# A new instruction order for a fused attention and gated-MLP block: logit sums in pairs, output projection last in three blocks

## The chip, the cores and the metric

The kernel runs on one core of one Trainium2 chip. The metric is the device time of one execution in microseconds (us). Three runs of the kernel before took 180.56, 180.65 and 180.72 us; the median is 180.65 us. The profiled execution is a run of its own and took 180.63 us, of which 179.4 us lie between its first and its last instruction (the span).

## The reference

The input x has 2048 positions of 512 features in bf16. Two branches read the same layer norm and are added to x:

```python
x = A_x
xn = _layernorm(x, axis=-1)
return x + _A_ref(xn, A_wqkv, A_wo) + _B_ref(xn, B_w_gate, B_w_up, B_w_down)
```

Branch A is attention with 32 heads of 16 features in which each position looks at itself and at seven positions behind it, two apart (`off = jnp.arange(8) * 2`); positions before the start are masked. After the softmax over the eight places and the weighted sum of v comes the projection with `wo` (512 x 512). Branch B is a gated MLP, `gelu(xn @ w_gate) * (xn @ w_up) @ w_down`, with 1376 hidden features.

## The kernel before

The 2048 positions are cut into four blocks (0 to 3) of 512 positions and sixteen tiles of 128. For each block the same tasks exist, and a task's name carries the block number:

- **Layer norm.** Blocks 0 and 1 mostly on VectorE (DVE), blocks 2 and 3 on ScalarE (ACT). The result xnT is transposed to [feature, position].
- **q, k, v** (`mm1_0_3_0` is block 1, q, group 3): four matmuls of 512 columns each on TensorE (PE) into one bank of PSUM; ACT copies the bank to SBUF (`evq`, `evk`, `evv`, L1029).
- **Attention logits.** DVE multiplies q with the eight shifted copies of k (`pr`, L1049, two instructions of 8192 elements per partition) and adds them up part of the way (`pa`, `pb`). The rest of the sum over features is done by PE with a 0/1 matrix: the task `er` (L1097), the *logit sums*. It works on 32 columns of the array at a time and also makes the last small part of the up projection (L1085), whose two results ACT copies out as `uev_10b` and `uev_10c` (L1292).
- **Softmax.** ACT copies the logits to SBUF (`lc`, L1120); DVE takes the maximum and subtracts it (`d1a` to `d1c`, `d2`); ACT takes the exponential (`exp`, L1143); DVE sums (`d4a` to `d4c`, L1151); ACT takes the logarithm (`ln`, L1161) and the exponential of its negative (`d5`, L1165), which is the reciprocal; DVE multiplies (`d6`, L1169). Four DMAs store the weights to a scratch tensor in HBM (`ss`) and four load them back spread over the heads (`sl`).
- **Weighted sum of v** on DVE (`pv`, L1199, `pw`, `pz`): `pz` writes the attention output OT of the block.
- **Gate and up projections** (`fg`, `fu`, ten pieces each and a rest): four matmuls of 512 columns into a bank; ACT reads the gate through gelu (`gelu`, L1247) and copies the up part (`uev`, L1254); DVE multiplies both (`h`, L1261) into HT.
- **Output** of each tile: one bank collects four matmuls OT x Wo and eleven HT x Wd (L1329). The parts are named `acca`, `accb`, `accd` (the Wd ones) and `accw` (the four Wo ones by themselves). With `WO_LAST` holding a block, the Wo matmuls of that block come at the end of the sum, as a task of their own; else they come at its start and the whole sum waits for `pz`. ACT copies the bank to the buffer OB (`fe`, L1362), DVE adds x (`fin`), a DMA stores (`sto`). In the last two tiles DVE reads the bank itself.

The order of the tasks on each engine is not found at run time: the table `ORDER` lists them by name, and the function `schedule` only deals out buffer slots in that order and the semaphore waits follow from the data. Each engine runs its list strictly in order. So do the DMAs, which all stand in the list of one queue, SP's. PSUM has eight banks in one pool; a matmul task waits until the bank that it is given has been read out.

ACT holds one set of function tables at a time. The line `e.preload_act_table_set("natural_log_exp_and_others")` (L1142) stands ahead of each `exp` and puts an instruction ACT_TABLE_LOAD there in every case; that set has the exponential and the logarithm. All other loads are put in when the program is built, where a function follows that is not in the set loaded last: for gelu, for `ln` and for `d5`. Plain copies (Identity) need none. In `schedule`, a switch is charged where the `table` of a task (`"gelu"`, `"exp"`) differs from the one before:

```python
G.task("act", "ln%d" % b, 0.21, mk_ln(), rd=[(it_ms, 0)], wr=[(it_ms, 0)], prio=base + 34, table="exp")
```

Of the kernel before, what the change touches and what calls it, by code (L numbers as in the profile page):

```python
# [96 lines left out]
class Graph:  # L97
# [251 lines left out]
    def report(self):  # L349
# [14 lines left out]
ORDER = {  # L364
# [14 lines left out]
    "act":  # L379
# [17 lines left out]
    "dve":  # L397
# [9 lines left out]
    "pool":  # L407
        "c_ones c_onef c_id c_vnpad c_idb c_eps c_mhalf c_e8a c_e8b c_e8c c_e8d c_ktpad c_mask0 c_mask1 c_utz sq8 "
# [9 lines left out]
}  # L418


# [16 lines left out]
def bass_parallel_sum__sliding_local_dilated__glu_gated_geglu__prompt_kernel(nc, A_x, A_wqkv, A_wo, B_x, B_w_gate, B_w_up, B_w_down, out, dbg=None, cfg=None):  # L437
    cfg = dict(cfg or {})
# [6 lines left out]
    JT = cfg.get("JT", 4.5)  # L445
    JLATE = cfg.get("JLATE", [8, 9])
    NMS = cfg.get("NMS", 1)
    NPB = cfg.get("NPB", 1)
    NPT = cfg.get("NPT", 4)
    NVN = cfg.get("NVN", 2)  # L450
    NOT = cfg.get("NOT", 2)
# [1 line left out]
    NHT = cfg.get("NHT", 2)  # L453
    NXR = cfg.get("NXR", 2)
    XRB = cfg.get("XRB", 2)
    NOB = cfg.get("NOB", 4)
    NDMASEM = cfg.get("NDMASEM", 24)
    QUOTAS = cfg.get("QUOTAS", dict(tp=2, qkv=2, lg=2, o=4, ffn=3,
                                    acc=2, acl=4))
# [7 lines left out]
    PPOW = cfg.get("PPOW", 4)  # L467
    FIN2 = cfg.get("FIN2", tuple(range(14)))
    PR_ADD3 = cfg.get("PR_ADD3", (0, 1, 2, 3))
    WO_LAST = cfg.get("WO_LAST", (3,))  # L470
    CHAIN_SHIFT = cfg.get("CHAIN_SHIFT", [0, 300, 600, 900])
    FFN_BASE = cfg.get("FFN_BASE", 500)
    FFN_STEP = cfg.get("FFN_STEP", 1000)
# [2 lines left out]
    NB, NP, NT = 4, 8, 16  # L476
    NJ = 11
    x2 = A_x[0]
    out2 = out[0]

    with contextlib.ExitStack() as es:
        def sb(name, shape, dt):
# [43 lines left out]
        GG = sb("GG", [128, NGG, 2, 512], BF)  # L526
# [3 lines left out]
        OB = sb("OB", [128, NOB, 512], BF)  # L530
        PS = es.enter_context(nc.psum_tensor("PS", [128, 4096], F32))
# [23 lines left out]
        P_gg = Pool("gg", NGG)  # L555
# [3 lines left out]
        P_ob = Pool("ob", NOB)  # L559
# [34 lines left out]
            out=cf[:, :], in_=cf[:, :], pattern=[[-1, 128]], compare_op=ALU.is_equal, fill=0.0, base=0,  # L594
# [7 lines left out]
            out=E8f[:, :], in_=E8f[:, :], pattern=[[-4, 32]], compare_op=ALU.is_ge, fill=0.0, base=0,  # L602
            channel_multiplier=1), rd=[I_E8f], wr=[I_E8f], prio=PC2)
        G.task("pool", "c_e8c", 0.25, lambda e: e.affine_select(
            out=E8f[:, :], in_=E8f[:, :], pattern=[[4, 32]], compare_op=ALU.is_ge, fill=0.0, base=3,
# [77 lines left out]
        for p in range(NP):  # L683
# [24 lines left out]
            for t2 in range(2):  # L708
                t = 2 * p + t2
# [209 lines left out]
        for b in range(NB):  # L919
# [383 lines left out]
            for ti in range(4):  # L1303
# [15 lines left out]
                for ci, (c0, c1) in enumerate(cparts):  # L1319
                    CW = c1 - c0  # L1320
                    sfx = "%d" % t if len(cparts) == 1 else "%d_%d" % (t, ci)
                    it_acc = Item("acc" + sfx, P_ps, "acl" if b in WO_LAST else "acc")
                    it_ob = Item("ob" + sfx, P_ob, "ob")

                    def mk_acc(ops, start, stop, ti=ti, it=it_acc, ith=it_ht, ito=it_ot, c0=c0, c1=c1, CW=CW):
                        def f(e):
# [33 lines left out]
                    if t in FIN2:  # L1360
# [5 lines left out]
                        def mk_fin(xr_of=xr_of, ito=it_ob):  # L1366
                            return lambda e: e.tensor_tensor(out=OB[:, ito.slot, :], in0=OB[:, ito.slot, :],
                                                             in1=xr_of(0, 512), op=ALU.add)
                        G.task("dve", "fin" + sfx, d_dve(CW, 0.52), mk_fin(), rd=[xrp], wr=[it_ob],
                               prio=base + 61)  # L1370
                    else:
                        def mk_fin(it=it_acc, xr_of=xr_of, ito=it_ob, c0=c0, c1=c1, CW=CW):
                            return lambda e: e.tensor_tensor(
                                out=OB[:, ito.slot, 0:CW], in0=PS[:, 512 * it.slot:512 * it.slot + CW],
                                in1=xr_of(c0, c1), op=ALU.add)
                        G.task("dve", "fin" + sfx, d_dve(CW), mk_fin(), rd=[it_acc, xrp], wr=[it_ob],
                               prio=base + 61)

                    def mk_so(t=t, it=it_ob, c0=c0, c1=c1, CW=CW):
                        return lambda e: e.dma_start(out2[128 * t:128 * t + 128, c0:c1], OB[:, it.slot, 0:CW])  # L1380
                    G.task("sp", "sto" + sfx, 0, mk_so(), rd=[it_ob], wr=[(I_out, (t, ci))], prio=base + 62,
                           nbytes=64 * CW)

# [43 lines left out]
```

## Time and profile before

| | before |
|---|---|
| median of three runs | 180.65 us |
| profiled execution | 180.63 us |
| its span | 179.4 us |
| TensorE (PE) busy | 174.6 us, 97% |
| VectorE (DVE) busy | 169.5 us, 94% |
| ScalarE (ACT) busy | 131.8 us, 73% |
| GpSimd (POOL) busy | 22.6 us, 13% |
| DMA engines, mean share | 37.5% on the one queue of the program |
| granted TensorE clock | 1.00 over the whole span |

Busy shares are means over the whole span. A line of the timeline gives the start and length of a stretch, the engine, the source line, the operation, the tiles (written <- read), the shape and the count; in brackets stands how long the engine was idle before it and what ended that. Consecutive instructions of DVE and ACT overlap in the records by about 0.1 us, so the step from one start to the next is what an instruction costs in a packed row.

### The profile page before, as it was taken

To read this page: it belongs to the slowest core of one execution; us is meant where nothing else is said; L and a number is where in the kernel's file an instruction comes from. 1 tells how busy PE (TensorE), PEld (TensorE's weight loads), DVE (VectorE), ACT (ScalarE), POOL (GpSimd) and SP (SyncE) were. 2 spreads that over 40 slices of the span, in tenths; PEclk is the share of its full clock that TensorE was granted. 3 is DMA by queue.
4 is the path that set the end of the run, shared out by engine and by line. 5 is a ranking of instruction groups with operands and counts; after the bars stand their busy time and mean duration, and the time that the engine had idled before them with its cause. 6 is when DMAs were issued, how large, how long until landed. Compare 5 with 4: busy or idle time off the path is not lost.

```text
span 179.4 us, 2670 instructions
## 1 busy us (share of the span) xinstructions
PE 174.6 (97%) x1007; PEld 88.4 (49%) x1024; DVE 169.5 (94%) x155; ACT 131.8 (73%) x262; POOL 22.6 (13%) x23
## 2 busy tenths in 40 slices
PE   7899999999999999999999999999999999999995
PEld 2797555444454455444444544444444444444453
DVE  3899999999999999999999999999899999999954
ACT  5689999999999999999766888734829796411031
POOL 6000350045000039117000000000000000000000
DMA  4995594640368110003660010053703067400123
GB/s 115 375 384 125 120 329 127 203 169 0 60 180 231 36 23 4 0 11 76 187 140 0 0 58 0 4 151 89 255 3 117 4 116 250 132 0 29 62 88 117
DMA packets 26988, 19.60 MB, mean 109 GB/s; under 512 B 13696, under 2 KB 24800, under 8 KB 26976
## 3 DMA queue, kind: packets, MB, share of 16 engines
q1 hardware_dynamic: 26976, 19.44, 37.5%
q8 instruction: 8, 0.13, 0.3%
q14 instruction: 4, 0.03, 0.1%
HBM read 14.71 MB, written 3.15 MB: 100 GB/s over the span
## 4 chain that ended last, share of the span: by engine, by line
PE 67%; ACT 16%; DVE 11%; DMA 2%; issue 1%; SPq 0%; DVEq 0%
PE PS L1329 25%; PE PS L1237 23%; PE PS L1018 10%; DVE UNI L1199 4%; ACT UU L1254 3%; PE PS L935 3%; ACT GG L1247 3%; DVE UNI L1208 2%; DMA Wqkv<-in_A_wqkv_dram 2%; ACT XS L774 2%; PE PS L993 1%; ACT L1247 1%; PE PS L1276 1%; DVE UNI L1214 1%; PE PS L949 1%
## 5 line engine op out<-in xcount | busy, mean ns | idle before, releaser
L1329 PE MATMUL PS<-Wd,HT 128*128 128x512 bf16 (+2 forms) x185 | 40.2, 366 | 0.1
L1237 PE MATMUL PS<-xnT,Wg 128*128 128x512 bf16 x156 | 38.9, 379 | 0.2
L1237 PE MATMUL PS<-xnT,Wu 128*128 128x512 bf16 x156 | 38.6, 379 | 0.2
L1199 DVE TENSOR_TENSOR UNI<-VN,PT 128x8192 f16<-128x8192 bf16 x8 | 35.4, 4420 | 0.9 <-DMA PT<-pt_scratch 0.9
L1049 DVE TENSOR_TENSOR UNI<-QT,KT 128x8192 f16<-128x8192 bf16 x8 | 35.3, 4418 | 0.0
L1018 PE MATMUL PS<-xnT,Wqkv 128*128 128x512 bf16 x141 | 32.7, 379 | 0.3 <-issue 0.2
L1329 PEld LDWEIGHTS PS<-Wd,HT 128*128 128x128 bf16 x187 | 17.9, 98 | 20.3
L1247 ACT ACTIVATE GG<-PS 128x512 bf16<-128x512 f32 x40 | 23.4, 612 | 5.8 <-DVE HT L1261 3.3
L781 POOL TENSOR_TENSOR sq<-vb,mhalf 128x2 bf16<-128x2 bf16 x4 | 19.7, 4925 | 60.4 <-ACT vb L778 60.4
L1254 ACT ACTIVATE UU<-PS 128x512 bf16<-128x512 f32 x40 | 23.4, 609 | 3.4 <-PE PS L1237 2.1
L1237 PEld LDWEIGHTS PS<-xnT,Wu 128*128 128x128 bf16 x160 | 15.6, 98 | 18.7 <-ACT GG L1247 0.3
L1237 PEld LDWEIGHTS PS<-xnT,Wg 128*128 128x128 bf16 x160 | 15.6, 98 | 18.6 <-ACT XIN L802 0.4
L1362 ACT ACTIVATE OB<-PS 128x512 bf16<-128x512 f32 x14 | 8.1, 593 | 22.4 <-PE PS L1329 20.6
L1018 PEld LDWEIGHTS PS<-xnT,Wqkv 128*128 128x128 bf16 x144 | 16.2, 114 | 15.1 <-ACT QT L1029 0.3
L1061 DVE TENSOR_TENSOR UNI<-UNI 128x8192 f16<-128x8192 f16 x4 | 17.7, 4420 | 0.0
L1208 DVE TENSOR_TENSOR UNI<-UNI 128x8192 f16<-128x8192 f16 x4 | 17.7, 4418 | 0.0
L1329 PE MATMUL PS<-Wo,OT 128*128 128x512 bf16 (+2 forms) x65 | 16.0, 366 | 0.2
L1261 DVE TENSOR_TENSOR HT<-GG,UU 128x1024 bf16<-128x1024 bf16 x20 | 13.4, 684 | 0.0
L1329 PEld LDWEIGHTS PS<-Wo,OT 128*128 128x128 bf16 x68 | 6.4, 98 | 7.6 <-issue 0.4
L1214 DVE TENSOR_TENSOR UNI<-UNI 128x4096 f16<-128x4096 f16 x4 | 9.1, 2286 | 0.0
L1068 DVE TENSOR_TENSOR UNI<-UNI 128x4096 f16<-128x4096 f16 x4 | 9.1, 2282 | 0.0
L1029 ACT ACTIVATE QT<-PS 128x512 bf16<-128x512 f32 x12 | 7.0, 610 | 1.2 <-PE PS L1018 1.2
(97 smaller groups left out, 176.3 us busy)
## 6 DMA issues: line engine op xcount, KB each, us to landing
PT<-pt_scratch SPq DMA_DIRECT2D x16, 256.0 KB, 4.3
out_dram<-OB SPq DMA_DIRECT2D x15, 128.0 KB, 1.7
XIN<-in_A_x_dram SPq DMA_DIRECT2D x12, 128.0 KB, 2.4
Wqkv<-in_A_wqkv_dram SPq DMA_DIRECT2D x3, 512.0 KB, 5.0
XIN<-in_A_x_dram SPq DMA_DIRECT2D x6, 256.0 KB, 5.0
Wg<-in_B_w_gate_dram SPq DMA_DIRECT2D x2, 640.0 KB, 5.9
Wu<-in_B_w_up_dram SPq DMA_DIRECT2D x2, 640.0 KB, 6.6
Wd<-in_B_w_down_dram SPq DMA_DIRECT2D x1, 1280.0 KB, 6.4
```

What stands on the lines that cost most here:

```text
L781: "pool", "sq%d" % t, 6.0, lambda e, t=t, n=n: e.tensor_tensor(out=sq[:, t:t + n], in0=vb[:, t:t + n], in1=mhalf[:, 0:n], op=ALU.pow),
L1018: ins = e.matmul(PS[:, 512 * it.slot:512 * it.slot + 512], lhsT=wcols(which, kt, g), rhs=xnT[:, itx.slot, kt, :], start=(kt == 0), stop=(k ...
L1049: return lambda e: e.tensor_tensor(out=UNI[:, it.slot:it.slot + 2, :, :], in0=bass.AP(QT, (itq.slot * 4 + 2 * h) * 512, [[NQT * 4 * 512, 1 ...
L1061: return lambda e: e.tensor_tensor(out=UNI[:, i0.slot:i0.slot + 2, :, :], in0=UNI[:, i0.slot:i0.slot + 2, :, :], in1=UNI[:, i1.slot:i1.slo ...
L1199: return lambda e: e.tensor_tensor(out=bass.AP(UNI, ito.slot * 4096, [[NUNI * 4096, 128], [2048, 4], [512, 4], [1, 512]]), in0=bass.AP(VN, ...
L1208: return lambda e: e.tensor_tensor(out=UNI[:, i0.slot:i0.slot + 2, :, :], in0=UNI[:, i0.slot:i0.slot + 2, :, :], in1=UNI[:, i1.slot:i1.slo ...
L1214: return lambda e: e.tensor_tensor(out=UNI[:, i0.slot, :, :], in0=UNI[:, i0.slot, :, :], in1=UNI[:, i0.slot + 1, :, :], op=ALU.add)
L1237: ins = e.matmul(PS[0:M, 512 * it.slot:512 * it.slot + 512], lhsT=Wx[:, kt, j * 128:j * 128 + M], rhs=xnT[:, itx.slot, kt, :], start=(kt = ...
L1247: return lambda e: e.activation(out=GG[:, ito.slot, q, :], in_=PS[:, 512 * it.slot:512 * it.slot + 512], func=ACTF.Gelu_apprx_tanh)
L1254: return lambda e: e.activation(out=UU[:, ito.slot, q, :], in_=PS[:, 512 * it.slot:512 * it.slot + 512], func=ACTF.Identity)
L1261: return lambda e: e.tensor_tensor(out=HT[:, ito.slot, j - 1:j + 1, :], in0=GG[:, ig.slot, :, :], in1=UU[:, iu.slot, :, :], op=ALU.mult)
L1329: ins = e.matmul(PS[:, 512 * it.slot:512 * it.slot + CW], lhsT=(OT[:, ito.slot, q, ti * 128:(ti + 1) * 128] if kind == "o" else HT[:, ith. ...
```

## The change

The table `ORDER` is replaced as a whole: the same tasks in another order on PE, ACT, DVE and SP (POOL is unchanged), with eight new tasks `accw0` to `accw7` that come from `WO_LAST`. `NPB` gives the softmax weights PB a second buffer, `NOB` takes one of four output buffers OB away, and the last two tiles write their output into a buffer of the gelu results (GG) in place of OB. No matmul, activation or vector operation is added or left out, apart from table loads.

```diff
-        "evq2_0_0 evq2_1_0 exp1 evq2_3_0 evk2_2_0 evk2_0_0 bnst14 ln1 halv2 bnst15 evk2_3_0 d5_1 uev1_7 sub12 "
+        "uev1_10c va14 uev1_2 exp1 uev1_5 gelu1_2 gelu1_4 gelu1_3 gelu1_5 sub14 norm12 sub15 evv1_2_0 norm13 "
...
-    NPB = cfg.get("NPB", 1)
+    NPB = cfg.get("NPB", 2)
...
-    NOB = cfg.get("NOB", 4)
+    NOB = cfg.get("NOB", 3)
...
-    WO_LAST = cfg.get("WO_LAST", (3,))
+    WO_LAST = cfg.get("WO_LAST", (0, 1, 3))
...
-                    it_ob = Item("ob" + sfx, P_ob, "ob")
+                    it_ob = Item("ob" + sfx, P_gg if t >= NT - 2 else P_ob, "ob")
+                    ob_of = ((lambda c0, c1, it=it_ob: GG[:, it.slot, 0, c0:c1]) if t >= NT - 2 else
+                             (lambda c0, c1, it=it_ob: OB[:, it.slot, c0:c1]))
...
-                                out=OB[:, ito.slot, 0:CW], in0=PS[:, 512 * it.slot:512 * it.slot + CW],
+                                out=ob_of(0, CW), in0=PS[:, 512 * it.slot:512 * it.slot + CW],
...
-                        return lambda e: e.dma_start(out2[128 * t:128 * t + 128, c0:c1], OB[:, it.slot, 0:CW])
+                        return lambda e: e.dma_start(out2[128 * t:128 * t + 128, c0:c1], ob_of(0, CW))
```

The lines of the changed kernel are one to three higher than those of the kernel before (L1143 for L1142, L1255 for L1254, L1332 for L1329).

**PE, the logit sums of blocks 0 and 1.** Before, the sums of block 1 (L1085 and L1097, 32 columns) stand alone among matmuls of 128 columns, as do those of block 0:

```order
L1237 MATMUL PS<-xnT,Wg 128x512 x4
L1085 MATMUL PS<-xnT,Wt 32x256 x16
L1097 MATMUL PS<-UNI,E 32x512 x8
L1237 MATMUL PS<-xnT,Wg 128x512 x4
L1018 MATMUL PS<-xnT,Wqkv 128x512 x8
```

Now those of block 0 (with the mask) are followed at once by those of block 1:

```order
L1019 MATMUL PS<-xnT,Wqkv 128x512 x20
L1086 MATMUL PS<-xnT,Wt 32x256 x16
L1093 MATMUL PS<-mask,const-bfloat16-1.0 32x4x16
L1098 MATMUL PS<-UNI,E 32x512 x4
L1093 MATMUL PS<-mask,const-bfloat16-1.0 32x4x16
L1098 MATMUL PS<-UNI,E 32x512 x4
L1086 MATMUL PS<-xnT,Wt 32x256 x16
L1098 MATMUL PS<-UNI,E 32x512 x8
L1019 MATMUL PS<-xnT,Wqkv 128x512 x4
```

Two entries into the 32-column form and two returns from it became one of each; the same holds for blocks 2 and 3.

**ACT, the exponential of block 1 (`exp1`).** Before, it stands among copies; the logarithm (L1161) and the second exponential (L1165) of the block follow with no gelu and no load between:

```order
L1142 ACT_TABLE_LOAD
L1143 ACTIVATE EX<-PB 128x1024
L1029 ACTIVATE QT<-PS 128x512
L1029 ACTIVATE KT<-PS 128x512 x2
L731 ACTIVATE XS,s<-XIN 128x512
L1161 ACTIVATE ms<-ms 128x128
L1037 ACTIVATE VN<-VN 128x4x16
L731 ACTIVATE XS,s<-XIN 128x512
L1029 ACTIVATE KT<-PS 128x512
L1165 ACTIVATE rc<-ms 128x128
```

Now it stands fifteen ACTIVATEs behind the exponential of block 0, with only copies, layer-norm work, `ln0` and `d5_0` between, and the gelus of block 1 follow:

```order
L1255 ACTIVATE UU<-PS 128x512
L1293 ACTIVATE UT<-PS 32x512
L775 ACTIVATE XS,s<-XIN,nmean 128x512
L796 ACTIVATE XIN<-XIN,nmean 128x512
L1293 ACTIVATE UT<-PS 64x256
L779 ACTIVATE vb<-s,eps 128x2
L1255 ACTIVATE UU<-PS 128x512
L1143 ACT_TABLE_LOAD
L1144 ACTIVATE EX<-PB 128x1024
L1255 ACTIVATE UU<-PS 128x512
L1248 ACT_TABLE_LOAD
L1248 ACTIVATE GG<-PS 128x512 x4
```

The load ahead of the exponential is still there, though the set is the one in use.

**ACT, the logarithm and reciprocal of block 1 (`ln1`, `d5_1`).** They are now behind gelus, and each has a load of its own:

```order
L1030 ACTIVATE VN<-PS 128x512 x2
L1162 ACT_TABLE_LOAD
L1162 ACTIVATE ms<-ms 128x128
L1030 ACTIVATE KT<-PS 128x512
L1030 ACTIVATE QT<-PS 128x512 x4
L1166 ACT_TABLE_LOAD
L1166 ACTIVATE rc<-ms 128x128
L1030 ACTIVATE KT<-PS 128x512 x2
```

In all, the list of ACT has 14 loads where it had 10: one gelu load less between the exponentials of blocks 0 and 1, three more for `ln1`, for `d5_1` and for the gelu behind them, and two more in block 3, where a gelu now stands between `ln3` and `d5_3`.

## Rows read from the trace of the kernel before

**Rows 1.** Windows: stretch, length, busy us (instructions) of PE, PEld, DVE, ACT, POOL; clock, DMA.
```profile
60.00:80.00 20.00, 19.89 (x93) 9.82 (x93) 19.98 (x16) 19.77 (x46) 6.89 (x1) 1.00 0.03 7
150.00:170.00 20.00, 19.89 (x93) 9.00 (x94) 20.00 (x14) 4.27 (x9) 0.00 (x0) 1.00 0.26 86
```

**Rows 2.** Timeline of PE around the logit sums of block 1: start, length, instruction.
```profile
54.89 1.03 PE L1237 MATMUL PS<-xnT,Wg 128*128 128x512 bf16 x4
55.85 0.62 PE L1085 MATMUL PS<-xnT,Wt 128*32 128x256 bf16 x16
56.30 0.61 PE L1097 MATMUL PS<-UNI,E 128*32 128x512 f16 x8
56.84 1.04 PE L1237 MATMUL PS<-xnT,Wg 128*128 128x512 bf16 x4
57.71 1.46 PE L1018 MATMUL PS<-xnT,Wqkv 128*128 128x512 bf16 x6
```

**Rows 3.** Groups by line, a table load of ACT: count, busy us, mean ns, idle before.
```profile
L1247 ACT ACT_TABLE_LOAD x5 | 6.4, 1283 | 0.1
```

**Rows 4.** Timeline of ACT, 66 to 82 us, around `exp1`, `ln1` and `d5_1`.
```profile
68.51 1.14 ACT L1029 ACTIVATE QT<-PS 128x512 bf16<-128x512 f32 x2
69.67 1.28 ACT L1142 ACT_TABLE_LOAD   x1
70.96 1.06 ACT L1143 ACTIVATE EX<-PB 128x1024 f16<-128x1024 bf16 x1
71.93 0.58 ACT L1029 ACTIVATE QT<-PS 128x512 bf16<-128x512 f32 x1
...
75.63 0.30 ACT L1165 ACTIVATE rc<-ms 128x128 f16<-128x128 f32 x1
...
77.01 0.71 ACT L802 ACTIVATE XIN<-XIN,rstd 128x512 bf16<-128x512 bf16 x1
```

**Rows 5.** Timeline of ACT, 57.8 to 67 us: a logit copy and a 64-row copy.
```profile
56.95 1.02 ACT L1120 ACTIVATE PB<-PS 128x1024 bf16<-128x1024 f32 x1
...
62.15 0.38 ACT L1292 ACTIVATE UT<-PS 64x256 bf16<-64x256 f32 x1
```

**Rows 6.** Timeline: where PE and DVE come to the packed part of block 0.
```profile
13.99 1.91 PE L993 MATMUL PS<-xnT,Wqkv 128*128 128x256 bf16 x16
...
15.64 4.42 DVE L1049 TENSOR_TENSOR UNI<-QT,KT 128x8192 f16<-128x8192 bf16 x1
```

**Rows 7.** Timeline of DVE, four stretches between 35 and 156 us.
```profile
44.65 0.69 DVE L1169 TENSOR_TENSOR PB<-EX,rc 128x1024 bf16<-128x1024 f16 x1 [0.26 <-ACT rc L1165]
...
78.39 0.68 DVE L1169 TENSOR_TENSOR PB<-EX,rc 128x1024 bf16<-128x1024 f16 x1
79.00 4.42 DVE L1049 TENSOR_TENSOR UNI<-QT,KT 128x8192 f16<-128x8192 bf16 x1
...
129.15 4.43 DVE L1199 TENSOR_TENSOR UNI<-VN,PT 128x8192 f16<-128x8192 bf16 x1 [0.88 <-DMA PT<-pt_scratch]
...
147.62 2.29 DVE L1214 TENSOR_TENSOR UNI<-UNI 128x4096 f16<-128x4096 f16 x1
149.95 1.23 DVE L1219 TENSOR_TENSOR OT<-UNI 128x2048 bf16<-128x2048 f16 x1
151.69 0.42 DVE L1367 TENSOR_TENSOR OB<-OB,XR 128x512 bf16<-128x512 bf16 x1
```

**Rows 8.** Timeline: first Wo matmuls of block 2, `pz3`, first Wo matmuls of block 3.
```profile
151.41 1.03 PE L1329 MATMUL PS<-Wo,OT 128*128 128x512 bf16 x4
...
170.72 1.22 DVE L1219 TENSOR_TENSOR OT<-UNI 128x2048 bf16<-128x2048 f16 x1
...
173.27 3.40 PE L1329 MATMUL PS<-Wo,OT 128*128 128x512 bf16 x15
```

**Rows 9.** Page, part 6: loads of the softmax weights and stores, count, KB, us to landing.
```profile
PT<-pt_scratch SPq DMA_DIRECT2D x16, 256.0 KB, 4.3
out_dram<-OB SPq DMA_DIRECT2D x15, 128.0 KB, 1.7
```

More of the change, by code (lines that the diff above doesn't have):

```diff
@@ L1371, in bass_parallel_sum__sliding_local_dilated__glu_gated_geglu__prompt_kernel, with mk_fin @@
                     else:
-                        def mk_fin(it=it_acc, xr_of=xr_of, ito=it_ob, c0=c0, c1=c1, CW=CW):
+                        def mk_fin(it=it_acc, xr_of=xr_of, ob_of=ob_of, c0=c0, c1=c1, CW=CW):
                             return lambda e: e.tensor_tensor(
-                                out=OB[:, ito.slot, 0:CW], in0=PS[:, 512 * it.slot:512 * it.slot + CW],
+                                out=ob_of(0, CW), in0=PS[:, 512 * it.slot:512 * it.slot + CW],
                                 in1=xr_of(c0, c1), op=ALU.add)
@@ L1377, in bass_parallel_sum__sliding_local_dilated__glu_gated_geglu__prompt_kernel, with mk_so @@
                                prio=base + 61)
-                    def mk_so(t=t, it=it_ob, c0=c0, c1=c1, CW=CW):
-                        return lambda e: e.dma_start(out2[128 * t:128 * t + 128, c0:c1], OB[:, it.slot, 0:CW])
+                    def mk_so(t=t, ob_of=ob_of, c0=c0, c1=c1, CW=CW):
+                        return lambda e: e.dma_start(out2[128 * t:128 * t + 128, c0:c1], ob_of(0, CW))
                     G.task("sp", "sto" + sfx, 0, mk_so(), rd=[it_ob], wr=[(I_out, (t, ci))], prio=base + 62,
```

87 rows, old and new, of the table ORDER are left out of this document.

## Prediction

> **What bounds the kernel now.** I read the windows first. From 60 to 80 us PE, DVE and ACT are all three busy for 19.8 of 20 us or more; from 150 to 170 us PE and DVE still are, and ACT has only 4.27 us of work [rows 1]. So there is no slack to win by filling gaps: PE runs through its list, DVE arrives with it, and ACT is full in the first half. Next I read the timeline of PE for places where it is busy without working at its step. Ordinary matmuls of 512 columns come every 0.216 us (four from 56.84 to 57.71, [rows 2]). Around the logit sums that is not so: the four gate matmuls from 54.89 us put the last start at 55.54, and the first 32-column matmul starts at 55.85, 0.31 us later; the two rounds of logit sums from 56.30 would let the next task start at 56.73, and it starts at 56.84. One visit to the 32-column form costs 0.095 + 0.105 = 0.20 us. Then I read the meetings of PE and DVE: the first Wo matmul of block 2 starts at 151.41 us, and `pz2`, which it needs, ends at 149.95 + 1.23 = 151.18 [rows 7, 8]; `pz3` ends at 171.94, the Wo matmuls of block 3 start at 173.27. Both paths are nearly equally long, so a microsecond lost on either becomes time.
>
> **What PE gains.** Four visits to the 32-column form become two: 2 x 0.20 = 0.40 us off PE. The number of matmuls is the same, and a Wo part split off costs nothing, since `accw` and `accd` have the same shape and step. If nothing else happened, the profiled 180.63 us (span 179.4 and 1.2 around it, as good as the median 180.65) would become 180.23.
>
> **What ACT pays.** A load takes 1.283 us [rows 3]; from the end of one ACTIVATE (69.65) to the start of the next (70.96) 1.31 us pass, and the overlap of 0.1 us that packed neighbours have is lost too: 1.4 us [rows 4]. The new list has four more. Those of block 3 are covered: `d6_3` stands behind `pv2_0` on DVE (4.3 us, [rows 7]), and `ln3`, load, gelu, load, `d5_3` take 0.3 + 1.3 + 0.6 + 1.3 + 0.3 = 3.8. Two are not covered, in my count: the one ahead of `exp1` and the one ahead of `d5_1`.
>
> First the meeting point. Both engines are packed from 15.7 us on: PE's gate projections start at 13.99 + 16 x 0.109 (half of 0.216, for 256 columns) = 15.73 [rows 6], 37 tasks follow until the logit sums (35 of 0.863, two of 0.87: 32.0), then `er0` with its entry 1.0: `er1` starts at T = 48.7. DVE starts its first product 0.3 late, since the last q matmuls of block 0 now stand one task later (15.94, [rows 6]), and has six steps of 4.34, two of 2.20, three of 0.61 and 0.3 in small ones: `pb1` ends at 48.5, 0.2 ahead of T.
>
> *The load at `exp1`.* PE from T to `fg1_9`: the logit sums and the return 0.98, 24 tasks of 0.863, 31 output matmuls of 0.216: T + 28.4. That task's bank is freed by `gelu1_6` on ACT. From `lc0` to `gelu1_6` ACT has 20 copies or gelus of 0.48, ten SBUF passes of 0.61, two `lc` of 0.92, two `exp` of 0.96, six UT copies (four of 0.40; the two of 32 rows I take at 0.6) and 0.9 of small ones: 23.2 [rows 4, 5], and three loads, 4.2. It begins between T + 0.2 (the sums of block 0 are read 0.04 us after their recorded end, [rows 2, 5]) and T + 1.1 (ACT is 99% busy and two copies late), and waits 0.4 to 0.8 us for PE and DVE at `gelu0_10`, `uev1_3` and `ln0`: done at T + 28.0 to 29.3. With 0.15 for release and weight load, PE waits between nothing and 1.05 us. I take 0.6, the late half, as ACT is full. Without the reload it would wait for nothing. DVE meets the same at `h1_1`: it comes at T + 22.3, `gelu1_3` is done at T + 22.0 to 23.3; I take 0.5.
>
> *The load at `d5_1`.* `evq3_2` copies what `mm3_0_2` made; counted like that, its record ends at T + 38.5 plus PE's delay. Then copy 0.04 + 0.60, load 1.31, `d5_1` 0.30: `d6_1` can start at T + 40.8 plus that delay. DVE has 39.5 us of steps from `pb1` to there and 0.6 for neighbours that depend on each other (a step of 0.04 after the end, where others overlap by 0.07, [rows 7]), so it comes at T + 39.9 plus its own: it waits 0.9. Before, this meeting had cover on both sides. PE meets the load as well: `evk3_3`, behind `d5_1`, frees the bank of `mm3_1_0`: it ends 0.04 + 0.60 + 1.31 + 0.20 + 0.60 = 2.75 after that record, plus 0.15, and PE is there after 2.43. PE waits 0.47.
>
> **Other parts.** DVE up to `pz2` has 0.33 us more work in its list (`h2_4`, `h3_10`, `fin6` for `h3_1`, `fin5`; a `fin` is 0.34, [rows 7]), three dependent neighbours less (-0.35), the later start (+0.3), and loses two old waits: `d6_0` 0.26 and `pv2_0` 0.88, 1.30 with the lost overlap [rows 7]. A new wait at `pv2_0` for the load of its weights is not shown; it lies between 0 and the old 0.88 (1.30 with the overlap). `sl3_3` stands behind `ldxr5` and `ldxr10`, which wait for `fin6`; two issues and 4.3 us to landing [rows 9] are 5.3, and DVE has 6.4 us of work from there to `pv3_1`: covered by 1.1. `sl1_2` and `sl1_1` stand behind `sto1`, which waits for `fin1`; `pa3`, `h1_4` and `pb3` (7.2 us) hide them. Three OB buffers let `fe8`, `fe10`, `fe12` and `fe13` wait for a store's landing; PE's last 3.2 us (tile 15, which uses GG) hide it, and without them it would cost up to 1.7 [rows 9]. The second PB costs nothing: without it `lc1` would wait for the stores of block 0.
>
> **The sum.** PE: -0.40 + 0.6 + 0.47 = +0.67. DVE reaches `pz2` at 151.18 + 0.33 - 0.35 + 0.3 - 1.30 + 0.5 + 0.9 = 151.56, or up to 152.5 with the DMA wait; PE reaches the Wo matmuls of block 2 at 151.41 + 0.67 = 152.08. So PE decides until that wait is over 0.4 us, and then DVE does, up to +1.25. After it DVE has 1.0 us less to do until `pz3` than before (`fin7` and `fin10` moved behind it), PE 1.8 less (`accd15_0`): `pz3` still comes first. I add 0.2 for the part of the cases in which DVE decides: +0.85, **181.5 us**. The likeliest case's own range is 181.0 to 181.9.
>
> What the Trainium skill says here stands by itself. "ScalarE: Activation LUTs", section "What ACT_TABLE_LOAD costs", gives about 1283 ns for the load, as the row, and a drain of about 1380 ns more, 2.66 us for a switch; the rows show the next ACTIVATE 1.31 us behind the last. By the page both waits on PE would grow by 1.35 us, and the time would be 184.2.
>
> **The rivals.**
> (1) Not slower: the loads are covered. If ACT comes to `lc0` at T + 0.2 and waits little, PE never meets it at `fg1_9`; and if the copies of block 3 run far enough ahead of PE, `d5_1` isn't late. For it speaks that ACT has idle time from 80 us on, against it that it has none between 60 and 80 [rows 1]. Both covered gives 180.25. It decides once ACT gains 0.6 us in one place and 0.5 in the other.
> (2) Only `d5_1` shows, because reloading the set in use costs little (no row has such a reload; 0 to 1.4): -0.40 + 0.47 + a little from DVE, 180.75.
> (3) DVE decides by DMA: `sl2_0` now has `sto3` and `ldxr11` ahead of it, and the wait at `pv2_0` stays at the old 0.88 or grows by half of that: 180.63 + 1.25 to 1.7, about 182.1. For it: DVE's only long wait before was this one. Against: the four stores of the weights now follow each other, so the loads go out sooner after `d6_2`.
> (4) Each load costs a drain as well, the page's figure: 184.2. All loads in the trace speak against it.
>
> **How the numbers follow.** Chances: forecast 0.55, (1) 0.12, (2) 0.14, (3) 0.12, (4) 0.02, something else 0.05. A measurement of this kernel tells about 0.2%, 0.36 us, from no change. Faster than that (under 180.3): 0.11, mostly (1). Within it (to 181.0): 0.17, most of (2), the low end of the forecast and a part of (1). Slower: 0.72. The range of 180.3 to 182.2 leaves out most of (1), half of (3) and (4).
>
> **What would show it.** Two stretches of 32-column matmuls with the usual step right before and after the pair; 14 table loads, one some 16 ACTIVATEs behind the first exponential; DVE idle 0.5 to 1 us before the product of L1170 in block 1, released by ACT's reciprocal; PE idle behind gelu copies near 77 us and behind a KT copy near 90 us. I am wrong if PE's step stays unbroken from 60 to 92 us, or if the 0.40 us do not appear.

## The result and the profile after

The changed kernel takes 182.50 us (median of five runs, 182.28 to 182.83), against 180.65 before: slower by 1.05%, ratio 1.0105 with an interval of 1.009 to 1.012. The forecast was 181.5, its range 180.3 to 182.2. The direction was right and the size was not: 1.85 us were lost where 0.85 were forecast, and the time lies above the top of the range.

The windows answer to [rows 1]; the columns are the same.

```profile
60.00:80.00 20.00, 19.16 (x87) 8.03 (x86) 18.39 (x22) 19.72 (x38) 2.86 (x1) 1.00 0.40 112
150.00:170.00 20.00, 20.00 (x94) 8.95 (x93) 20.00 (x13) 6.14 (x12) 0.00 (x0) 1.00 0.19 59
```

From 60 to 80 us ACT is as full as before, but PE lost 0.7 us and DVE 1.6. From 150 us on both are packed again. So the loss sits in the middle. The weight loads of PE show where: a group that starts late has in brackets how long the loader was idle and for whom.

```profile
48.30 0.34 PEld L1086 LDWEIGHTS PS<-xnT,Wt 128*32 128x32 bf16 x16 [0.41 <-ACT QT L1030]
...
50.19 0.58 PEld L1019 LDWEIGHTS PS<-xnT,Wqkv 128*128 128x128 bf16 x4 [0.42 <-ACT XS L732]
...
70.15 2.06 PEld L1332 LDWEIGHTS PS<-Wd,HT 128*128 128x128 bf16 x11 [1.23 <-ACT UU L1255]
...
76.94 0.55 PEld L1238 LDWEIGHTS PS<-xnT,Wu 128*128 128x128 bf16 x4 [0.41 <-ACT GG L1248]
78.03 0.58 PEld L1019 LDWEIGHTS PS<-xnT,Wqkv 128*128 128x128 bf16 x4 [0.55 <-ACT GG L1248]
79.13 0.33 PEld L1238 LDWEIGHTS PS<-xnT,Wg 128*128 128x128 bf16 x3 [0.52 <-ACT GG L1248]
...
92.03 0.58 PEld L1019 LDWEIGHTS PS<-xnT,Wqkv 128*128 128x128 bf16 x4 [0.70 <-ACT KT L1030]
...
153.42 0.55 PEld L1332 LDWEIGHTS PS<-Wo,OT 128*128 128x128 bf16 x4 [0.38 <-DVE OT L1220]
```

The two logit sums from 48.30 to 50.19 are the pair: one entry and one return where [rows 2] had these for each block. The idle times here are the loader's, which runs ahead; what the matmuls lose is less and comes from the starts: a task of 0.863 us that takes 1.095 has lost 0.23. Counted so, PE loses 0.95 us up to the task at 70.15 (`accd1`, its bank freed by the copy `uev1_5`) and 0.56 more up to `fg1_9` at 79.13 (its bank freed by `gelu1_6`): 1.51 in all. At 92.03 (`mm3_1_0_0`) it loses 0.40, and at 153.42 (Wo of block 2) 0.06; in a second profile of the same kernel (e0 below) the last is 0.13.

What ACT does ahead of 70.15, and ahead of 92.03, answers to [rows 4]:

```profile
65.19 0.71 ACT L796 ACTIVATE XIN<-XIN,nmean 128x512 bf16<-128x512 bf16 x1
65.93 0.38 ACT L1293 ACTIVATE UT<-PS 64x256 bf16<-64x256 f32 x1
66.33 0.30 ACT L779 ACTIVATE vb<-s,eps 128x2 bf16<-128x2 f32 x1
66.65 0.60 ACT L1255 ACTIVATE UU<-PS 128x512 bf16<-128x512 f32 x1
67.26 1.28 ACT L1143 ACT_TABLE_LOAD   x1
68.56 1.06 ACT L1144 ACTIVATE EX<-PB 128x1024 f16<-128x1024 bf16 x1
69.52 0.58 ACT L1255 ACTIVATE UU<-PS 128x512 bf16<-128x512 f32 x1
70.12 1.28 ACT L1248 ACT_TABLE_LOAD   x1
...
89.27 0.60 ACT L1030 ACTIVATE QT<-PS 128x512 bf16<-128x512 f32 x1 [1.13 <-PE PS L1019]
89.89 1.28 ACT L1166 ACT_TABLE_LOAD   x1
91.18 0.31 ACT L1166 ACTIVATE rc<-ms 128x128 f16<-128x128 f32 x1
91.40 1.06 ACT L1030 ACTIVATE KT<-PS 128x512 bf16<-128x512 f32 x2
```

The reload ahead of `exp1` takes 1.28 us though the set is in place, and `uev1_5`, for which PE waits, stands right behind. The load ahead of `d5_1` delays the reciprocal and the KT copy `evk3_3`. DVE, the answer to [rows 7], waits in four places between 60 and 92 us, all behind ACT and three of them behind one of the two loads:

```profile
63.38 0.69 DVE L1170 TENSOR_TENSOR PB<-EX,rc 128x1024 bf16<-128x1024 f16 x1 [0.50 <-ACT rc L1166]
...
69.65 0.42 DVE L1152 TENSOR_TENSOR SU<-EX 128x512 f16<-128x512 f16 x1 [0.63 <-ACT EX L1144]
...
73.02 1.29 DVE L1262 TENSOR_TENSOR HT<-GG,UU 128x1024 bf16<-128x1024 bf16 x2 [0.41 <-ACT GG L1248]
...
91.53 0.69 DVE L1170 TENSOR_TENSOR PB<-EX,rc 128x1024 bf16<-128x1024 f16 x1 [0.94 <-ACT rc L1166]
```

To take the start of the kernel out of the comparison, the table counts from PE's first gate weight load to the first weight load of its last task. In three profiles of before and in two of after this stretch repeats within 0.07 us, and the start in front of it does not; what follows the last task's weight load takes 2.3 us in every profile. The two profiles of the kernel with neither load differ by 0.44, which e3 explains.

| kernel | first gate load | last task | between | against before |
|---|---|---|---|---|
| before; two more profiles of it | 15.63; 15.71; 15.66 | 177.07; 177.16; 177.11 | 161.45 | |
| after | 16.13 | 179.09 | 162.96 | +1.51 |
| after, again (e0) | 15.75 | 178.78 | 163.03 | +1.58 |
| no reload at `exp1` (e1) | 15.77 | 177.37 | 161.61 | +0.16 |
| one load for `ln1` and `d5_1` (e2) | 15.53 | 178.03 | 162.49 | +1.04 |
| neither (e3; e8) | 15.86; 15.55 | 177.38; 176.64 | 161.52; 161.08 | +0.07; -0.37 |
| two small copies out (e4) | 15.76 | 177.35 | 161.59 | +0.14 |
| both pairs apart, no loads (e5) | 15.54 | 178.91 | 163.37 | +1.92 |
| one pair apart (e7) | 15.46 | 177.99 | 162.53 | +1.08 |
| the same, ACT's copies moved (e9) | 15.86 | 177.13 | 161.28 | -0.17 |
| reload where ACT is idle (e10) | 15.46 | 177.12 | 161.66 | +0.21 |

### The profile page after: what moved, and what is told of

Its sections match the earlier page's. It is cut to its first block, busy times and chain, and to the rows that moved or that the text cites. A ratio compares the mean times of both kernels' runs of the same rounds, so it can differ in the third digit from the quotient of the medians.

```text
span 181.4 us, 2684 instructions
## 1 busy us (share of the span) xinstructions
PE 177.2 (98%) x1024; PEld 88.9 (49%) x1024; DVE 169.7 (94%) x155; ACT 136.6 (75%) x266; POOL 13.5 (7%) x23
## 4 chain that ended last, share of the span: by engine, by line
PE 80%; ACT 15%; DMA 3%; issue 1%; SPq 0%; DVE 0%
PE PS L1238 30%; PE PS L1332 25%; PE PS L1019 15%; PE PS L936 3%; DMA Wqkv<-in_A_wqkv_dram 3%; PE PS L994 2%; ACT UU L1255 2%; ACT GG L1248 2%; PE PS L1277 1%; ACT L1143 1%; ACT UT L1293 1%; ACT EX L1144 1%; PE PS L950 1%; PE PS L1086 1%; ACT XIN L796 1%; PE PS L1098 1%
## 5 line engine op out<-in xcount | busy, mean ns | idle before, releaser
L1332 PE MATMUL PS<-Wd,HT 128*128 128x512 bf16 (+2 forms) x187 | 40.6, 367 | 0.7 <-ACT UU L1255 0.7
L1238 PE MATMUL PS<-xnT,Wu 128*128 128x512 bf16 x160 | 39.9, 379 | 0.0
L1019 PE MATMUL PS<-xnT,Wqkv 128*128 128x512 bf16 x144 | 34.6, 380 | 0.3 <-ACT KT L1030 0.2
L1332 PEld LDWEIGHTS PS<-Wd,HT 128*128 128x128 bf16 x187 | 17.8, 98 | 21.5 <-ACT UU L1255 1.6
L1255 ACT ACTIVATE UU<-PS 128x512 bf16<-128x512 f32 x40 | 24.1, 625 | 4.3 <-PE PS L1238 4.2
L1332 PE MATMUL PS<-Wo,OT 128*128 128x512 bf16 (+2 forms) x68 | 16.0, 367 | 0.0
L782 POOL TENSOR_TENSOR sq<-vb,mhalf 128x2 bf16<-128x2 bf16 x4 | 10.7, 2673 | 55.0 <-ACT vb L779 55.0
L1332 PEld LDWEIGHTS PS<-Wo,OT 128*128 128x128 bf16 x68 | 6.5, 98 | 7.5 <-DVE OT L1220 0.4
L1030 ACT ACTIVATE QT<-PS 128x512 bf16<-128x512 f32 x12 | 7.6, 645 | 1.2 <-PE PS L1019 1.1
```

Source lines behind the costliest of these rows:

```text
L782: "pool", "sq%d" % t, 6.0, lambda e, t=t, n=n: e.tensor_tensor(out=sq[:, t:t + n], in0=vb[:, t:t + n], in1=mhalf[:, 0:n], op=ALU.pow),
L1019: ins = e.matmul(PS[:, 512 * it.slot:512 * it.slot + 512], lhsT=wcols(which, kt, g), rhs=xnT[:, itx.slot, kt, :], start=(kt == 0), stop=(k ...
L1238: ins = e.matmul(PS[0:M, 512 * it.slot:512 * it.slot + 512], lhsT=Wx[:, kt, j * 128:j * 128 + M], rhs=xnT[:, itx.slot, kt, :], start=(kt = ...
L1255: return lambda e: e.activation(out=UU[:, ito.slot, q, :], in_=PS[:, 512 * it.slot:512 * it.slot + 512], func=ACTF.Identity)
L1332: ins = e.matmul(PS[:, 512 * it.slot:512 * it.slot + CW], lhsT=(OT[:, ito.slot, q, ti * 128:(ti + 1) * 128] if kind == "o" else HT[:, ith. ...
```

## The experiments

**e0, the changed kernel again.** No edit.

> The changed kernel once more, unaltered. Of the 1.99 us between the two profiled executions 0.50 lie ahead of the first gate matmul (16.13 against 15.63 us from the start), where both kernels issue the same instructions in the same order until 11.7 us: the first load of Wqkv lands at 6.47 us instead of 5.99. Theory A (this part varies from execution to execution): the load lands anywhere from 5.9 to 6.5 us in this profile and the median stays at 182.5 give or take 0.2. Theory B (this part belongs to the changed kernel, by another layout of SBUF): it lands at 6.4 to 6.6 us again, and the first gate matmul starts at 16.1 again.

Median 182.38 us (181.95 to 182.99; ratio 1.0089, 1.0072 to 1.0107). The first gate load starts at 15.75 us and the first load of Wqkv lands at 5.72: theory A. Over eleven profiles of the changed kernel and its variants the start lies between 15.46 and 16.13, with a median of 15.75; three profiles of before give 15.63 to 15.71. Of the 0.50 us at the start of the profile compared above 0.12 are left in this one.

**e1, no reload at `exp1`.**

```diff
...
-                    e.preload_act_table_set("natural_log_exp_and_others")
+                    if b != 1:
+                        e.preload_act_table_set("natural_log_exp_and_others")
                     return e.activation(out=EX[:, :], in_=PB[:, it.slot, :], func=ACTF.Exp)
```

> The changed kernel without the table load ahead of the exponential of block 1 (the set it needs is in place). Theory 1 (ACT is late by its own sum, and the reload, 1.31 us and 0.1 of lost overlap, is on the path): of the 1.52 us that PE waits between 64 and 80 us about 0.1 stay, the load at d5_1 still costs 0.4, and the time is 182.5 - 1.4 = 181.1 (180.8 to 181.4). Theory 2 (what makes ACT late is that both logit copies and the copies of both rests now come at once behind the pair, load or no load): PE keeps at least half of the wait, 181.8 or more. Theory 3 (DVE or the landing of softmax weights takes over once PE is let go): PE waits at the Wo matmuls of block 2, 181.6 to 182.0.

Median 180.85 us (ratio to before 1.0011, 0.9999 to 1.0023). ACT runs through, and PE's two output tasks `acca0` and `accd1` follow each other as one group of 20 weight loads, with no wait for `uev1_5`:

```profile
66.28 0.60 ACT L1256 ACTIVATE UU<-PS 128x512 bf16<-128x512 f32 x1
66.77 1.05 ACT L1145 ACTIVATE EX<-PB 128x1024 f16<-128x1024 bf16 x1
67.72 0.59 ACT L1256 ACTIVATE UU<-PS 128x512 bf16<-128x512 f32 x1
```

```profile
66.93 4.00 PEld L1333 LDWEIGHTS PS<-Wd,HT 128*128 128x128 bf16 x20 [0.35 <-ACT UU L1256]
```

The stretch falls by 163.03 - 161.61 = 1.42 us, nearly the whole of PE's wait between 64 and 80 us: of 1.51 us 0.08 are left. Theory 1; theory 2 falls, and so does theory 3, since PE waits at the Wo matmuls of block 2 no longer than in e0 (0.14 and 0.13 us).

**e2, one load for `ln1` and `d5_1`.**

```diff
...
+                    if b == 1:
+                        e.preload_act_table_set("natural_log_exp_and_others")
+                    return e.activation(out=msv(), in_=msv(), func=ACTF.Ln)
...
```

> The changed kernel with the set that holds both functions loaded ahead of the logarithm of block 1, so that the exponential d5_1 behind it needs no load of its own. Theory 1: d6_1 on DVE loses most of its wait of 0.94 us, PE loses its 0.40 us at mm3_1_0_0, and the time falls by 0.4, to 182.1 (181.9 to 182.3). Rival: evk3_3_0 was late by the copies ahead of it and not by the load; no change, 182.5.

Median 181.66 us (ratio 1.0052, 1.004 to 1.0065). The reciprocal follows the q copy at once, and `d6_1` on DVE has no wait:

```profile
88.67 0.60 ACT L1030 ACTIVATE QT<-PS 128x512 bf16<-128x512 f32 x1 [1.13 <-PE PS L1019]
89.16 0.30 ACT L1170 ACTIVATE rc<-ms 128x128 f16<-128x128 f32 x1
```

```profile
89.91 0.69 DVE L1174 TENSOR_TENSOR PB<-EX,rc 128x1024 bf16<-128x1024 f16 x1
```

The stretch falls by 0.54 us: the 0.40 at `mm3_1_0_0`, and 0.13 at the Wo matmuls of block 2, where DVE no longer comes late. The median fell by 0.7 against e0, to below the range expected; the profiled execution starts 0.22 us sooner than that of e0 (15.53 against 15.75), which is the size of the rest, though for the median that isn't shown.

**e3 and e8, neither load.** Both edits.

> Both edits: 12 table loads. Theory 1: the parts add up, 182.5 - 1.4 - 0.4 = 180.7 (180.4 to 181.0), which is what the pairs of logit sums give (-0.40 against before) plus 0.5 at the start, if that is the changed kernel's own, or 180.3 if it is not. Theory 3 (DVE takes over): 181.2 or more, with PE waiting for the attention output of block 2.

> e3_neither_load once more, on the same chip as e7_one_pair_apart: 180.36 give or take 0.15, faster than the kernel before by 0.1 to 0.2%.

Medians 180.36 us (ratio 0.9975, 0.9955 to 0.9995) and 180.56 (0.9991, 0.9976 to 1.0007). The parts add up: 163.03 - 1.42 - 0.54 = 161.07, measured 161.08 in e8. In e3's profile DVE waited 0.6 us at 30.9 us for a square root that POOL computes, and the sums of block 1 came 0.41 later behind those of block 0 than in e8, which has no such wait: nearly all of the 0.44 between the two. Against before, 161.08 is 0.37 us less, where 0.40 were forecast for the pairs alone. The gain in the median is 0.1 to 0.3 us; in e8, whose median is 0.05 above the range expected, it can't be told from no change.

**e4, two small copies out.** `uev1_10a` and `uev1_10c` are left out, of the list of ACT and of the program, and with them a part of the up projection of block 1.

```diff
+                if b == 1 and nm in "ac":
+                    continue
                 G.task("act", "uev%d_10%s" % (b, nm), 0.61 if nm == "a" else 0.40, ...
```

> The changed kernel without two of the small ACT copies, uev1_10a (32x512) and uev1_10c (64x256), whose results are left out of the gated MLP. All table loads stay. Theory 1a (each of these copies also takes the overlap of 0.1 us from the ACTIVATE ahead of it and the one behind): without them ACT comes 0.73 + 0.53 = 1.26 us sooner to the exponential of block 1, and of the 1.52 us that PE waits between 64 and 80 us 0.2 to 0.3 stay; time 182.4 - 1.25 = 181.15. Theory 1b (they cost what the prediction put them at, 0.60 + 0.40 = 1.00): 0.5 us of the wait stay. Theory 2 (PE waits for something that ACT's sum does not set): no change.

Median 181.02 us (ratio 1.0018, 1.0005 to 1.0031). All loads stand, and of PE's wait between 64 and 80 us only 0.08 is left (the stretch is 161.59, as in e1). The stretch of ACT ahead of the reload, without the copies:

```profile
62.89 0.58 ACT L1255 ACTIVATE UU<-PS 128x512 bf16<-128x512 f32 x1
63.36 0.71 ACT L775 ACTIVATE XS<-XIN,nmean 128x512 bf16<-128x512 bf16 x1
...
64.07 0.71 ACT L796 ACTIVATE XIN<-XIN,nmean 128x512 bf16<-128x512 bf16 x1
64.68 0.29 ACT L779 ACTIVATE vb<-s,eps 128x2 bf16<-128x2 f32 x1
64.87 0.58 ACT L1255 ACTIVATE UU<-PS 128x512 bf16<-128x512 f32 x1
65.47 1.28 ACT L1143 ACT_TABLE_LOAD   x1
```

From the up copy `uev1_4` to `uev1_2` 1.98 us pass; with the copies it was 3.39 (63.26 to 66.65 in the changed kernel):

```profile
63.26 0.58 ACT L1255 ACTIVATE UU<-PS 128x512 bf16<-128x512 f32 x1
63.86 0.59 ACT L1293 ACTIVATE UT<-PS 32x512 bf16<-32x512 f32 x1
64.47 0.72 ACT L775 ACTIVATE XS<-XIN,nmean 128x512 bf16<-128x512 bf16 x1
```

The two copies cost 1.41 us, not 1.00 as the prediction had them and more than the 1.26 of theory 1a, since `uev1_2` behind `va14` follows closer as well. Theory 1a in kind, its size 0.15 short. It also shows that the wait of PE is a matter of ACT's sum: taking out the reload or taking out the same time in copies gives the same stretch.

**e5, both pairs apart, on top of e3.**

```diff
-... mm2_1_1_0 er0_3 er1_3 ...
+... er0_3 mm2_1_1_0 er1_3 ...
...
-... fu2_3 er2_3 er3_3 ...
+... er2_3 fu2_3 er3_3 ...
```

> e3_neither_load with one task of four 512-column matmuls between the logit sums of blocks 0 and 1 and one between those of blocks 2 and 3 (a q projection and an up projection change places with the first sums of each pair); everything else stays. Theory 1 (a visit to the 32-column form costs 0.20 us wherever it stands, and PE is the bound of that kernel): 2 x 0.20 = 0.40 us more, 180.36 + 0.4 = 180.75. Rival (the pair's gain was given back elsewhere, or the visit costs nothing when the neighbours are ordinary matmuls): within 0.1 of 180.36.

Median 182.39 us (ratio 1.01, 1.0085 to 1.0115): neither. The first visit costs 0.2 us as it should, but two new waits came. The k projection that now stands between the sums (the text above calls it a q projection) is 1.1 us later, and the first product of block 2 on DVE waits for its copy:

```profile
49.60 4.43 DVE L1050 TENSOR_TENSOR UNI<-QT,KT 128x8192 f16<-128x8192 bf16 x1 [0.81 <-ACT KT L1030]
```

The other is in blocks 2 and 3; e7 has it alone.

**e7 and e9, the sums of blocks 2 and 3 apart.** e7 makes the second half of e5's edit; e9 moves one copy on ACT as well:

```diff
-... uev2_3 evv2_3_0 lc2 uev2_10c lc3 ...
+... evv2_3_0 lc2 uev2_3 uev2_10c lc3 ...
```

> e3_neither_load with the logit sums of blocks 2 and 3 alone taken apart: the up projection fu2_3 stands between them instead of ahead of them. Those of blocks 0 and 1 stay together, so that no q projection of block 2 comes later (in e5_pairs_apart one did, and DVE waited 0.8 us for it at the products of block 2). Theory 1: one more visit to the 32-column form, 0.20 us more between 105 and 111 us and in the time, 180.36 + 0.20 = 180.56, with no new wait of PE. Rival (taking the pair apart is worth what e5 lost, since the sums of block 3 then wait for DVE): 0.6 us or more.

> e7_one_pair_apart with the ACT copy uev2_3 moved behind the logit copy lc2. In e7 the sums of block 3 waited 1.18 us for a bank that evv2_3 reads out, and that copy stood behind uev2_3, which waits for the up projection now put between the sums: a new wait made by the order of ACT and not by the form of the matmuls. Theory 1 (the visit alone costs 0.20 us): without that wait the stretch is 0.20 longer than in e3_neither_load, time about 180.45 + 0.2 = 180.65. Rival (the sums need to be neighbours for another reason, DVE or the banks): 1 us or more again, 181.5.

e7: median 181.79 us (ratio 1.0065, 1.0041 to 1.0088); e9: 180.40 (0.999, 0.9978 to 1.0002). In e7 the sums of block 3 wait for a bank that a v copy reads out, and that copy is queued behind `uev2_3`, which waits for the task put in between:

```profile
106.60 1.04 PE L1243 MATMUL PS<-xnT,Wu 128*128 128x512 bf16 x4
108.81 0.62 PE L1086 MATMUL PS<-xnT,Wt 128*32 128x256 bf16 x16 [1.18 <-ACT VN L1030]
```

With ACT's order mended the wait is gone:

```profile
106.99 1.04 PE L1243 MATMUL PS<-xnT,Wu 128*128 128x512 bf16 x4
107.96 0.62 PE L1086 MATMUL PS<-xnT,Wt 128*32 128x256 bf16 x16
```

The stretch is 161.28 - 161.08 = 0.20 us longer than e8's: theory 1, one visit. The medians can't show 0.20, since the start varies by more.

**e10, a reload where ACT is idle.** e3 with `if b in (1, 3):` in the edit of e2.

> e3_neither_load with one more load of the set in use, put ahead of the logarithm of block 3, where ACT is idle for 1.6 us in that kernel. Theory 1 (a reload takes 1.31 us of ACT wherever it stands, and costs time only where ACT is full): the gap ahead of the logarithm shows the load, PE and DVE as before, time the same as e3_neither_load's, 180.45 give or take 0.15. Rival (a load stops more than ACT's own stream, or costs the same everywhere): 1 us or more, as at the exponential of block 1.

Median 180.71 us (ratio 1.0015, 1.0004 to 1.0026); the stretch is 0.58 us longer than e8's. Neither theory. ACT is idle for 1.62 us in front of the logarithm, but the load doesn't use that time; it waits for the same DVE result as the logarithm behind it. First e8, then e10:

```profile
129.81 0.60 ACT L1030 ACTIVATE VN<-PS 128x512 bf16<-128x512 f32 x1 [0.23 <-PE PS L1019]
132.03 0.31 ACT L1166 ACTIVATE ms<-ms 128x128 f32<-128x128 f32 x1 [1.62 <-DVE ms L1153]
```

```profile
129.70 0.60 ACT L1030 ACTIVATE VN<-PS 128x512 bf16<-128x512 f32 x1 [0.22 <-PE PS L1019]
131.92 1.28 ACT L1165 ACT_TABLE_LOAD   x1 [1.62 <-DVE ms L1153]
133.22 0.31 ACT L1166 ACTIVATE ms<-ms 128x128 f32<-128x128 f32 x1
```

So all behind it is 1.3 us later, of which PE sees 0.55 as a wait for an output copy (137.60 us). A reload that is asked for inside a waiting task costs what the queue behind it has no slack for; the idle time ahead of it was no cover.

**The kernel before, twice more.**

> The kernel before, unaltered, for another look at its start. In the five profiles of the changed kernel and its variants the first gate matmul starts at 15.53 to 16.13 us, as the first load of Wqkv lands at 5.67 to 6.47; in the one profile of before at 15.63. Theory A (chance): it starts anywhere between 15.5 and 16.1 here too. Theory B (the changed kernel's start is later): 15.6 again.

> The same once more: theory A 15.5 to 16.1 us, theory B 15.6.

180.70 and 180.63 us; the first gate load at 15.71 and 15.66 us, the stretch 161.45 both times. The three starts of before lie within 0.09 us, as theory B has it. Of the eleven of the changed kernel and its variants (15.46 to 16.13) five are sooner than all three, so they aren't later as a rule; that is theory A. The two of the changed kernel itself, 15.75 and 16.13, are both later than before, and two can't decide.

## Why the prediction was right in kind and wrong in size

The stretch is 1.51 to 1.58 us longer. By the runs that is -0.40 for the pairs, +1.42 for the reload at `exp1`, and +0.54 for the load at `d5_1`.

- **The pairs, -0.40: right.** e9 prices one visit at 0.20, and e8, which has the new order without the two loads, is 0.37 shorter than before. The gain was there all along, under 1.96 us of waits.
- **The reload at `exp1`, forecast 0.6, measured 1.42: the step that failed.** It is the term for ACT from `lc0` to `gelu1_6`, put at 23.2 us and three loads, 27.4 in all, and done at T + 28.0 to 29.3, with the wait of PE taken at the late half of 0 to 1.05. In the changed kernel T (the first matmul of `er1`), `lc0` and `gelu1_6` are these:

```profile
49.18 0.66 PE L1086 MATMUL PS<-xnT,Wt 128*32 128x256 bf16 x16
...
50.08 1.96 ACT L1121 ACTIVATE PB<-PS 128x1024 bf16<-128x1024 f32 x2
...
78.44 0.64 ACT L1248 ACTIVATE GG<-PS 128x512 bf16<-128x512 f32 x1
```

`lc0` began at T + 0.90, within what was allowed (0.2 to 1.1), and `gelu1_6` ended at T + 29.90, 0.6 behind the late end. The one wait of ACT in between cost 0.27 (0.4 to 0.8 had been allowed). So what was too low is the sum of its steps: 28.7 against 27.4. Read from the trace, 0.9 of these 1.3 us is overlap lost in seven places by 0.11 to 0.15 each: six where an instruction is followed by one of the small UT copies (`uev0_10a` to `uev1_10c`), and one behind `va14`. Another 0.3 is in the small instructions, which were put at 0.9 and take 1.2 even without lost overlap; and 0.16 is that `gelu1_6` itself was counted as a step of 0.48, where its end comes 0.64 after its start. The UT copy was shown in [rows 5] without its neighbours; in the kernel before they leave a gap of 0.02 us on either side of it, and neither overlaps it:

```profile
61.92 0.20 ACT L774 ACTIVATION_READ_ACCUMULATOR XS<-XIN,nmean 128x1 f32 x1
...
62.55 0.60 ACT L1029 ACTIVATE VN<-PS 128x512 bf16<-128x512 f32 x1
```

The prediction read one side only, as a step of 0.40 from one start to the next; that the instruction ahead of the copy loses its overlap too was left out. e4 measures this for two of the six copies: 1.41 us where 1.00 was put. PE's own date was right within 0.1. In e1, without the wait, T is 48.81 and `fg1_9` starts at T + 28.52, where 28.4 was put:

```profile
48.81 0.66 PE L1086 MATMUL PS<-xnT,Wt 128*32 128x256 bf16 x16
...
77.34 1.04 PE L1239 MATMUL PS<-xnT,Wg 128*128 128x512 bf16 x4
```

In the changed kernel it starts 0.05 us after the end of `gelu1_6` (0.15 was put for the release), at T + 29.95: 1.43 later, and by the stretch 1.42.

- **The load at `d5_1`: right.** PE waits 0.40 (0.47 forecast) and `d6_1` 0.94 (0.9 forecast). DVE then decides at the Wo matmuls of block 2 by 0.06 to 0.13, where 0.2 had been added for it; that this is so near is luck, as the next point shows.
- **DVE's old waits: wrong.** That of `d6_0` was said to go; it became 0.50, because `d5_0` is behind the same late ACT. That of `pv2_0` shrank to 0.2 to 0.3 in the changed kernel, so rival (3), the DMA, did not decide. `h1_1` waited 0.41 (0.5 forecast); the 0.63 of `d4a_1`, which reads what `exp1` writes, had not been named. With these waits `pz2` ends at 153.05 us in e0 (it starts at 151.83 and takes 1.22), whose first gate load is 0.12 later than before: 1.4 later than the 151.56 of the forecast. PE comes to the Wo matmuls of block 2 0.8 later than its 152.08 as well, by the reload, and the 0.5 that DVE had in hand is used up; hence so little shows. None of these waits held PE up before: in e1 those of `d4a_1` and `h1_1` are gone, and PE's wait at these Wo matmuls is the same.
- **Block 3's loads and the output copies: covered, as said.** In e0 PE's step is unbroken from `er3` to the Wo matmuls of block 2, and ACT's 17 us of waiting for stores cost PE nothing.
- **Rivals.** (1) falls by the size of the waits. (2) assumed that reloading the set in use is cheap; it takes 1283 ns, as any other load. (4) is refuted in the new places too: 1.31 us pass from the end of the last ACTIVATE to the next one, at the reload (67.25 to 68.56) and at the load for `d5_1` (89.87 to 91.18). The Trainium skill ("ScalarE: Activation LUTs", section "What ACT_TABLE_LOAD costs") adds a drain of about 1380 ns for every switch to a different set. The load for `d5_1` is such a switch and shows none; of a reload of the set in use, to which the prediction applied the same figure, the section doesn't speak.
- **What stays open.** About 1.55 of the 1.85 us are on PE's stretch, and what follows it is equal in all profiles. That leaves the start for the rest, which varied by 0.67 us over eleven profiles; whether the changed kernel starts later on average, these runs can't tell.

## What to carry to other kernels

Where an engine is busy for 99% of a stretch, add up its list neighbour by neighbour, with the step on both sides of each odd instruction, and take the late end: here the 1.3 us left out of the sum more than doubled the wait of the engine that it serves, from 0.6 to 1.42. A function load is an entry in the list like any other; check where a new order puts loads that the planner doesn't count, and load once the set that holds both functions. An order is a whole of four lists: taking one pair apart on PE alone cost 1.25 us through a copy on ACT besides the visit's 0.20, and nothing but the visit once that copy was moved.

## What was new about the hardware

- The ACTIVATEs over 32 or 64 partitions (32x512, 64x256) did not overlap their neighbours. In both kernels all twelve of these copies start 0.02 us or more after the end of the one ahead, and the next starts 0.02 or more after theirs, where neighbours over 128 partitions mostly start 0.1 before that end. Whether the number of partitions is the cause, or the place they start at, was not tried.
- ACT_TABLE_LOAD of the set in use takes 1283 ns, and one that is asked for inside a task waited for what the task waits for (e10, where ACT was idle for 1.62 us ahead of it).
